# Block 0 of a fused S5 scan and GEGLU kernel: the second token tile goes last and is turned by DMA instead of on TensorE

## The chip, the cores and the metric

The kernel runs on one core of one Trainium2 chip. A core has TensorE (PE, matrix products; its loads of the stationary operand are listed apart as PEld), VectorE (DVE), ScalarE (ACT), GpSimd (POOL) and SyncE (SP), which here issues nearly all DMAs. Sixteen DMA engines move the data. TensorE's results land in PSUM, which has eight banks of 128 x 512 floats. The metric is the device time of one execution in microseconds; lower is better. The three runs of the kernel before took 176.82, 176.93 and 176.80 us, so the median is 176.82.

## The reference, cut to what matters

```
xn = (x - mean(x)) / sqrt(var(x) + 1e-5)                 # x: 2048 tokens x 512
dt = exp(log_dt);  Lam_bar = exp(dt * Lam)               # 512 complex states
Bu = xn @ (((Lam_bar - 1) / Lam)[:, None] * (B_re + i B_im)).T
h[t] = Lam_bar * h[t-1] + Bu[t]                          # scan over the tokens
A = 2 * real(h @ (C_re + i C_im).T) + xn * Dskip
B = (gelu(xn @ w_gate) * (xn @ w_up)) @ w_down           # hidden width 1376
out = x + A + B                                          # bf16
```

The result is the input plus a state-space branch plus a gated feed-forward branch, both fed by the layer-normed input.

## The kernel before, in words

The 2048 tokens are four blocks of 512, and a block is four tiles of 128 tokens. All of it lives in one large SBUF tensor, the arena, so the profile shows most operands as "arena". The hidden width 1376 is cut into tiles 0 to 9 of 128 columns and tile 10 of 96. The state branch makes B products (`BU`, L749), a scan on VectorE (`CHAIN`), and C products in the same PSUM bank as the down projection (`DN`, L885).

A program of operations with their reads and writes is built first. A planner orders them: TensorE and SyncE keep the order in which the operations are written; on VectorE, ScalarE and GpSimd a list scheduler with estimated durations and due times picks the order, and `order_behind` and `ch` pin some of them in a chain. Waits follow from the reads and writes.

*Two forms of the feed-forward products.* In the usual form (`GU`, L843) the weights are stationary and the normed, turned tokens `XNT` (features on partitions) stream through, giving hidden columns on partitions and 512 tokens in a row. `GU_rest` (L817) does the 96-column tile with the tokens stationary. Block 0 begins before its layer norm is known. There the tokens are only centred (L951, L962), turned on TensorE by `cent_T` (L684, four 128 x 128 turns a tile, copied to `XC` by ScalarE, L689), and kept stationary while gate and up weights stream (`GT_k`, L701, one k slice at a time as weights arrive; `GT_mm`, L712, all four k slices). The factor 1/sqrt(var) is put in later, by ScalarE's gelu (L721) and VectorE's product (L724). The result `H0`, tokens on partitions, covers hidden columns 0 to 895 in four units u of 256, 256, 256 and 128 columns, and is turned by DMA (`H0_T`, L730). Tiles 7 to 10 of block 0 are done in the usual form and need the normed tokens, `XNT[0]`, which `TR(0)` turns by DMA (L736, one DMA a token tile).

*Order on TensorE in block 0:* warm-up, turns and k slices of token tiles 0, 1 and 2 for units 0 and 1 (banks 0 to 5), the turn of token tile 3, then `GT_mm` for (token tile 3, units 0 and 1) and for all tiles with units 2 and 3, then `GU` tiles 7 to 9 (tile 7 in two token halves, so that its first half needs only the turned tokens of tiles 0 and 1), `GU_rest`, the B products of block 0, and the B products of block 1, whose first four units are cut in token halves too.

*Order on SyncE:* x tiles and the k slices of the first 512 gate and up columns (L497, L488); gate and up columns 512 to 895 (L493, 384 columns, rows of 768 bytes); gate and up columns 896 to 1375 (480 columns, rows of 960 bytes); the turn of the parameters (L515); `TR(0)`, four turns; x of block 1 (L482); the turns of B_re and B_im out of HBM (L526); Dskip (L535); x of block 2; `TR(1)`, four turns; and later `H0_T`, `TR(2)`, C, w_down and x of block 3. In block 0, ScalarE's queue loads two of the x tiles and the parameters.

*Order on VectorE around the change:* statistics of the x tiles, centring, root and reciprocal (L621, L627), the norms of `TR(0)`'s tiles (L634), the products of the token-stationary form (L724), and then the statistics of block 1. `GATE["hm"]` holds block 1's statistics behind the last product before them.

Of the kernel before, what the change touches and what calls it, by code (L numbers as in the profile page):

```python
# [365 lines left out]
def build(nc, ins, out):  # L366
    with ExitStack() as es:
# [16 lines left out]
        FC = [(0, 512), (512, 896), (896, F)]  # L384
        WGc = [Buf("WGc%d" % i, "sbx", 10 * i, 10 * i + 1) for i in range(KD + 2)]
        WUc = [Buf("WUc%d" % i, "sbx", 100 + 10 * i, 101 + 10 * i) for i in range(KD + 2)]
        wdeps = lambda Wc, ft: Wc[0:KD] if ft < 4 else [Wc[KD + (ft > 6)]]
# [30 lines left out]
        XT0 = XTk[0]  # L418
# [77 lines left out]
        def ld_x0(j, queue="sync", after=()):  # L496
            return S.dma(lambda e, j=j: e.dma_start(X[j].ap, x2[128 * j:128 * (j + 1), :]), 128 * 1024, writes=[X[j]], tag="ld_x0", queue=queue, after=after)  # L497
# [7 lines left out]
        ld_w(WG, WGc, ins["B_w_gate"], 1)  # L505
        ld_w(WU, WUc, ins["B_w_up"], 1)
# [22 lines left out]
        def load_W():  # L529
            ld_w(WG, WGc, ins["B_w_gate"], 2)  # L530
            ld_w(WU, WUc, ins["B_w_up"], 2)
# [172 lines left out]
        def GT_mm(j, u, bank):  # L704
            f0, f1 = FR[u]
            w = f1 - f0
            dst = PS[bank][:, 0:2 * w].rearrange("p (w f) -> p w f", w=2)

            def f(e):
                ins_ = None  # L710
                for k in range(KD):
                    ins_ = e.matmul(dst, XCd(j, k), WGU[:, :, k, f0:f1], start=(k == 0), stop=(k == KD - 1))  # L712
                return ins_
            PE(f, d_pe([2 * w] * KD), wdeps(WGc, 2 * u) + wdeps(WUc, 2 * u) + XCs[j], [BANK[bank]], "GT")

        def GT_evac(j, u, bank):
            f0, f1 = FR[u]
            w = f1 - f0
            GATE["nh"] = kk = (GATE["nh"] + 1) % 3
            sc, rb = rss[j]  # L720
            GATE["last_gelu"] = S.order_behind(ACT(lambda e: e.activation(GG[kk].ap[:, 0:w], PS[bank][:, 0:w], ACTF.Gelu_apprx_tanh, scale=sc),  # L721
                                                   d_act(w, 1), [BANK[bank], rb], [GG[kk]], "gelu"), GATE.get("last_gelu"))
            hp = Buf("H0_%d_%d" % (j, u), "sb", H0[j].lo + 2 * f0, H0[j].lo + 2 * f1)
            GATE["hm"] = S.order_behind(V(lambda e: e.scalar_tensor_tensor(H0[j].ap[:, f0:f1], PS[bank][:, w:2 * w], sc, GG[kk].ap[:, 0:w], ALU.mult, ALU.mult),  # L724
                                          d_dve_1x(w), [BANK[bank], GG[kk], rb], [hp], "hmul"), GATE.get("hm"))

        def H0_T():
            for j in range(4):
                wr = [Buf("HT0_%d_%d" % (ft, j), "sb", HTt[0][ft].lo + 256 * j, HTt[0][ft].lo + 256 * (j + 1)) for ft in range(7)]
                S.dma(lambda e, j=j: e.dma_start_transpose(HT[0].ap[:, 0:7, 128 * j:128 * (j + 1)], H0[j].ap),  # L730
                      3.5 * 224 * 1024, reads=[H0[j]], writes=wr, tag="tr_h0", issue=2100.0)

        def TR(b, js=range(4)):
            for j in js:
                tt = 4 * b + j
                S.dma(lambda e, b=b, j=j, tt=tt: e.dma_start_transpose(  # L736
                    XNT[b].ap[:, :, 128 * j:128 * (j + 1)], XN[tt % 8].ap),
                    1.6 * 128 * 1024, reads=[XN[tt % 8]], writes=[XTk[b][j]], tag="tr_x%d" % b, issue=1280.0)
# [67 lines left out]
        def GU_rest(b):  # L806
            k2, ft = b % 2, KF - 1
            f0, m = 128 * ft, FROWS[ft]
            for i in range(2):
# [10 lines left out]
                PE(f, d_pe([2 * m] * 8), [WGc[KD + 1], WUc[KD + 1]] + XTr(b), [BANK[bank]], "GR%d" % b)  # L820
# [11 lines left out]
        def GU(b, fts=None, halved=()):  # L832
# [14 lines left out]

            for ft in fts:
# [4 lines left out]
                banks[ft] = (next_bank(), next_bank())  # L853
                bg, bu = banks[ft]
                kk = (KF * b + ft) % 3
                for j0, j1 in (((0, 2), (2, 4)) if ft in halved else ((0, 4),)):
                    for (W, Wc, bank) in zip((WG, WU), (WGc, WUc), banks[ft]):
                        mm(ft, W, Wc, bank, 128 * j0, 128 * j1, XTr(b)[j0:j1])
# [10 lines left out]
        def DN(b, split=False, tail=None):  # L869
# [4 lines left out]
            def seed(j, c0=0, c1=D):  # L874
                tt, bank = 4 * b + j, banks[j]
# [22 lines left out]
            def store(j, c0=0, c1=D):  # L898
                tt = 4 * b + j
# [3 lines left out]
                V(lambda e: e.tensor_tensor(OUTB[ko].ap[:, c0:c1], PS[bank][:, c0:c1], XD[tt].ap[:, c0:c1], ALU.add),  # L903
                  d_dve_1x(c1 - c0), [BANK[bank], XD[tt]], [ob], "evO")
# [90 lines left out]
        ch(*stats(0, 3)); ch(sub(3))  # L995
        ch(recip(qb0, rq0))
        op, mn3, qb3, rq3 = root(0, 3, 4)
        ch(op)
        rss = [(rq0.ap[:, i:i + 1], rq0) for i in range(3)] + [(rq3.ap, rq3)]
        for j in range(2):  # L1000
            ch(norms(0, [j], mn0, rq0, 0))
        ch(recip(qb3, rq3))
        TR(0, [0, 1])
        ks(1, 2, [0, 1])
        ks(2, 2, [0, 1])
        for j in range(3):
            GT_k(3, j, 0, [0, 1])
            if j == 0:
                cent_T(3, 0, 4, 6)
# [3 lines left out]
        for (j, u), bank in zip([(3, 0), (3, 1), (0, 2), (0, 3), (1, 2), (1, 3), (2, 2), (2, 3), (3, 2), (3, 3)],  # L1013
                                (6, 7, 0, 1, 2, 3, 4, 5, 0, 7)):
            GT_mm(j, u, bank)
            GT_evac(j, u, bank)
        rstate["n"] = 2
        norms(0, [2], mn0, rq0, 0)
        norms(0, [3], mn3, rq3, 3)
        TR(0, [2, 3])  # L1020
        ld_x(1)
# [6 lines left out]
        GU(0, [7, 8, 9, 10], halved=[7])  # L1028
# [82 lines left out]
```

## Time and profile before

| | |
|---|---|
| median of 3 runs | 176.82 us (176.80 to 176.93) |
| the profiled execution | 177.26 us, span 175.9 us |
| instructions | 2549 |
| TensorE busy | 172.8 us, 98% of the span, 903 matmuls |
| VectorE, ScalarE, GpSimd busy | 159.7, 95.8, 10.7 us |
| HBM read, written | 6.46 MB, 2.10 MB |
| granted TensorE clock | 1.00 |

How to read it: the span is the time from the first to the last instruction of the profiled execution. Busy times are sums by engine; DMA-issuing instructions aren't counted in them. SPq is SyncE's queue, that is the instructions that issue DMAs; a DMA's landing is the time from its issue until its data is there. The chain of work that ended last is followed back from the last instruction: each step leads to what released it, or to the instruction before it on its engine. L numbers are lines of the kernel before; the changed kernel's lines lie 1 to 19 further down.

### The profile page before, as it was taken

What the parts mean: (1) busy time and instruction counts of PE and PEld (TensorE: products, weight loads), DVE (VectorE), ACT (ScalarE), POOL (GpSimd) and SP (SyncE); (2) the same over time, 40 slices, a digit from 0 to 9 for tenths busy, and PEclk for the clock granted to TensorE, in tenths of its full rate; (3) what the DMA queues carried; (4) which work ended last, traced back from release to release, by engine and by line L of the source; (5) the groups of instructions that cost most, each with busy time, mean ns of one, the idle gap of its engine ahead of it and who ended that gap; (6) DMA issues with size and microseconds to landing.
All of it is one profiled execution on the core that took longest, in us unless ns stands there. A gap on an engine that the chain in (4) does not pass through costs nothing.

```text
span 175.9 us, 2549 instructions
## 1 busy us (share of the span) xinstructions
PE 172.8 (98%) x903; PEld 85.4 (49%) x903; DVE 159.7 (91%) x279; ACT 95.8 (54%) x187; POOL 10.7 (6%) x24
## 2 busy tenths in 40 slices
PE   7999999999999999999999999999999999999995
PEld 2645664744544444444644444444464444444454
DVE  6797999987999989889899999989999899999941
ACT  5367668999766899383676793000667970000000
POOL 3132120211000000002200000000000000000000
DMA  5999989975899000002015000002004000000311
GB/s 144 281 322 154 216 136 203 174 132 114 162 270 270 11 0 2 0 30 75 18 33 112 5 0 4 0 0 89 30 0 34 0 0 0 0 0 4 119 62 60
DMA packets 32421, 14.36 MB, mean 82 GB/s; under 512 B 23737, under 2 KB 32409, under 8 KB 32409
## 3 DMA queue, kind: packets, MB, share of 16 engines
q1 hardware_dynamic: 31952, 13.84, 36.9%
q10 hardware_dynamic: 456, 0.36, 0.6%
q8 instruction: 7, 0.11, 0.3%
q14 instruction: 6, 0.04, 0.1%
HBM read 6.46 MB, written 2.10 MB: 49 GB/s over the span
## 4 chain that ended last, share of the span: by engine, by line
PE 95%; DMA 2%; SPq 1%; issue 0%; DVE 0%
PE PS L885 37%; PE PS L843 32%; PE PS L749 16%; PE PS L712 4%; PE PS L817 3%; PE PS L701 2%; DMA arena<-in_B_w_up_dram 2%; SPq L488 1%; PE PS L684 0%; SPq L497 0%; DVE arena L903 0%
## 5 line engine op out<-in xcount | busy, mean ns | idle before, releaser
L885 PE MATMUL PS<-arena 128*128 128x512 bf16 (+3 forms) x323 | 66.2, 366 | 0.0
L843 PE MATMUL PS<-arena 128*128 128x512 bf16 (+1 forms) x272 | 58.1, 373 | 0.0
L885 PEld LDWEIGHTS PS<-arena 128*128 128x128 bf16 (+1 forms) x323 | 30.8, 98 | 35.2
L843 PEld LDWEIGHTS PS<-arena 128*128 128x128 bf16 x272 | 26.5, 98 | 29.5
L787 DVE TENSOR_TENSOR_SCAN arena<-arena 128x512 bf16<-128x512 f32 x32 | 38.9, 1256 | 0.0
L859 ACT ACTIVATE arena<-PS 128x512 bf16<-128x512 f32 x33 | 19.8, 599 | 26.2 <-DVE arena L903 16.7
L749 PE MATMUL PS<-arena 128*128 128x512 bf16 (+1 forms) x144 | 28.3, 355 | 0.1
L863 ACT ACTIVATE arena<-PS 128x512 bf16<-128x512 f32 x33 | 19.8, 599 | 5.4 <-PE PS L843 5.4
L749 PEld LDWEIGHTS PS<-arena 128*128 128x128 bf16 x144 | 14.0, 98 | 13.7 <-DMA arena<-arena 0.6
L877 ACT ACTIVATE PS<-arena 128x512 f32<-128x512 bf16 (+2 forms) x17 | 9.6, 582 | 19.7 <-DVE arena L903 19.0
L758 ACT ACTIVATE arena<-PS 128x512 bf16<-128x512 f32 x32 | 17.6, 597 | 1.6 <-PE PS L749 1.6
L903 DVE TENSOR_TENSOR arena<-PS,arena 128x512 bf16<-128x512 f32 (+2 forms) x17 | 10.9, 654 | 6.4 <-PE PS L885 6.4
L865 DVE TENSOR_TENSOR arena<-arena 128x512 bf16<-128x512 bf16 x33 | 13.2, 419 | 2.1 <-ACT arena L863 2.0
L776 DVE TENSOR_TENSOR arena<-arena 128x4096 bf16<-128x4096 bf16 (+1 forms) x5 | 9.2, 1859 | 0.4 <-ACT arena L611 0.4
L799 DVE TENSOR_TENSOR arena<-arena 128x4096 bf16<-128x4096 bf16 x4 | 9.2, 2291 | 0.1
L774 DVE TENSOR_TENSOR arena<-arena 128x4096 bf16<-128x4096 bf16 (+1 forms) x5 | 9.2, 1861 | 0.0
L800 DVE TENSOR_TENSOR arena<-arena 128x4096 bf16<-128x4096 bf16 x4 | 9.1, 2287 | 0.0
L615 DVE BATCH_NORM_STATS2 arena<-arena 128x6 f32<-128x512 bf16 x12 | 7.8, 685 | 0.9 <-DMA arena<-in_A_x_dram 0.7
L721 ACT ACTIVATE arena<-PS,arena 128x256 bf16<-128x256 f32 (+1 forms) x16 | 6.5, 450 | 3.3 <-DVE arena L621 1.5
L712 PE MATMUL PS<-arena 128*128 128x512 bf16 (+1 forms) x40 | 7.1, 336 | 0.0
L701 PE MATMUL PS<-arena 128*128 128x256 bf16 (+1 forms) x36 | 6.2, 308 | 0.2 <-DMA arena<-in_B_w_up_dram 0.2
L724 DVE SCALAR_TENSOR_TENSOR arena<-PS,arena 128x256 bf16<-128x256 f32 (+1 forms) x16 | 6.2, 444 | 0.0
(95 smaller groups left out, 124.2 us busy)
## 6 DMA issues: line engine op xcount, KB each, us to landing
out_dram<-arena SPq DMA_DIRECT2D x15, 128.0 KB, 1.7
arena<-in_A_x_dram SPq DMA_DIRECT2D x3, 512.0 KB, 6.3
arena<-in_B_w_down_dram SPq DMA_DIRECT2D x1, 1280.0 KB, 8.8
arena<-in_B_w_gate_dram SPq DMA_DIRECT2D x4, 128.0 KB, 3.4
arena<-in_B_w_up_dram SPq DMA_DIRECT2D x4, 128.0 KB, 3.6
arena<-in_B_w_gate_dram SPq DMA_DIRECT2D x1, 480.0 KB, 6.8
arena<-in_B_w_up_dram SPq DMA_DIRECT2D x1, 480.0 KB, 7.6
arena<-arena SPq DMA_TRANSPOSE x25, 3.3
```

The lines of the kernel that those rows point to most:

```text
L701: PE(lambda e: e.matmul(dst, XCd(j, k), WGU[:, ws[0]:ws[-1] + 1, k, f0:f1], start=first, stop=k == KD - 1, skip_group_check=True), d_pe([w ...
L712: ins_ = e.matmul(dst, XCd(j, k), WGU[:, :, k, f0:f1], start=(k == 0), stop=(k == KD - 1))
L749: ins_ = e.matmul(PS[bank][:, 128 * j0:128 * j1], BBT[c][dk].ap[:, 128 * s:128 * (s + 1)], XNT[b].ap[:, dk, 128 * j0:128 * j1], start=(dk ...
L758: GATE["evBu"] = ACT(lambda e, bank=bank, k3=k3, s=s, c=c: e.activation(SSc[k3][s][c].ap, PS[bank][:, :], ACTF.Copy), d_act(512), [BANK[ba ...
L787: V(lambda e, g=g, rb=rb, init=init: e.tensor_tensor_scan(g.ap, rb, g.ap, init, ALU.mult, ALU.add), d_dve_scan(512), [g, PA[RRr]] + ([CARc ...
L843: ins_ = e.matmul(PS[bank][0:m, c0:c1], W.ap[:, dk, 128 * ft:128 * ft + m], XNT[b].ap[:, dk, c0:c1], start=(dk == 0), stop=(dk == KD - 1))
L859: GATE["last_gelu"] = ACT(lambda e, bg=bg, kk=kk, m=m: e.activation(GG[kk].ap[0:m, :], PS[bg][0:m, :], ACTF.Gelu_apprx_tanh), d_act(512), ...
L863: ACT(lambda e, bu=bu, kk=kk, m=m: e.activation(UPB[kk].ap[0:m, :], PS[bu][0:m, :], ACTF.Copy), d_act(512), [BANK[bu]], [UPB[kk]], "evU")
L865: V(lambda e, kk=kk, m=m, ft=ft, k2=k2: e.tensor_tensor(HTt[k2][ft].ap[0:m, :], GG[kk].ap[0:m, :], UPB[kk].ap[0:m, :], ALU.mult), d_dve_tt ...
L877: ACT(lambda e: e.activation(PS[bank][:, c0:c1], X[tt].ap[:, c0:c1], ACTF.Copy), d_act(c1 - c0), [X[tt]], [BANK[bank]], "seed")
L885: ins_ = e.matmul(PS[bank][:, c0:c1], l_[:, 128 * j:128 * (j + 1)], r_[:, c0:c1], start=False, stop=last and n == len(ops) - 1, skip_group ...
L903: V(lambda e: e.tensor_tensor(OUTB[ko].ap[:, c0:c1], PS[bank][:, c0:c1], XD[tt].ap[:, c0:c1], ALU.add), d_dve_1x(c1 - c0), [BANK[bank], XD ...
```

## The change

1. The x tiles of block 0 are loaded into slots in the token order 0, 2, 3, 1 (`TOK`). Slots 0 to 2 (token tiles 0, 2, 3) are centred and turned on TensorE as before. Slot 3 (token tile 1) is no longer centred and turned on TensorE: its token-stationary products read the normed tokens in `XNT[0]`, turned by DMA, and its gelu and product take no factor.
2. `TR(0)` is cut up: turns of slots 0 and 3 (token tiles 0 and 1), then the load of the last 480 up columns, then x of block 1, then the turns of slots 1 and 2.
3. The 384-column chunk of gate and up becomes two, of 256 and 128 columns (rows of 512 and 256 bytes).
4. The order of `GT_mm` changes: unit 2 of slots 0, 1, 2, unit 3 of slots 0, 1, 2, then all four units of slot 3.
5. `GU` tiles 7, 8 and 9 are all cut in token halves, and the first halves of all three come before the second halves.

```diff
-        FC = [(0, 512), (512, 896), (896, F)]
+        FC = [(0, 512), (512, 768), (768, 896), (896, F)]
...
-        XT0 = XTk[0]
+        TOK = (0, 2, 3, 1)
+        XT0 = [XTk[0][t] for t in TOK]
...
         def load_W():
-            ld_w(WG, WGc, ins["B_w_gate"], 2)
-            ld_w(WU, WUc, ins["B_w_up"], 2)
+            ld_w(WG, WGc, ins["B_w_gate"], 3)
...
                 for k in range(KD):
-                    ins_ = e.matmul(dst, XCd(j, k), WGU[:, :, k, f0:f1], start=(k == 0), stop=(k == KD - 1))
+                    xs = XCd(j, k) if j < 3 else XNT[0].ap[:, k, 128 * TOK[j]:128 * (TOK[j] + 1)]
+                    ins_ = e.matmul(dst, xs, WGU[:, :, k, f0:f1], start=(k == 0), stop=(k == KD - 1))
...
+            def both(ft, j0, j1):
+                for (W, Wc, bank) in zip((WG, WU), (WGc, WUc), banks[ft]):
+                    mm(ft, W, Wc, bank, 128 * j0, 128 * j1, XTr(b)[j0:j1])
+
+            for ft in halved:
+                banks[ft] = (next_bank(), next_bank())
+            for ft in halved:
+                both(ft, 0, 2)
             for ft in fts:
...
+                if ft in halved:
+                    both(ft, 2, 4)
+                else:
+                    banks[ft] = (next_bank(), next_bank())
+                    both(ft, 0, 4)
...
-        ch(*stats(0, 3)); ch(sub(3))
-        ch(recip(qb0, rq0))
+        ch(*stats(0, 3))
         op, mn3, qb3, rq3 = root(0, 3, 4)
         ch(op)
-        rss = [(rq0.ap[:, i:i + 1], rq0) for i in range(3)] + [(rq3.ap, rq3)]
-        for j in range(2):
-            ch(norms(0, [j], mn0, rq0, 0))
+        ch(recip(qb0, rq0))
+        rss = [(rq0.ap[:, i:i + 1], rq0) for i in range(3)]
+        ch(norms(0, [0], mn0, rq0, 0))
+        ch(norms(0, [1], mn0, rq0, 0))
         ch(recip(qb3, rq3))
-        TR(0, [0, 1])
+        ch(norms(0, [3], mn3, rq3, 3))
+        TR(0, [0, 3])
+        ld_w(WU, WUc, ins["B_w_up"], 3)
+        ld_x(1)
+        TR(0, [1])
         ks(1, 2, [0, 1])
         ks(2, 2, [0, 1])
         for j in range(3):
             GT_k(3, j, 0, [0, 1])
-            if j == 0:
-                cent_T(3, 0, 4, 6)
             GT_k(3, j, 1, [0, 1])
             for u in range(2):
                 GT_evac(j, u, acc(j, u))
-        for (j, u), bank in zip([(3, 0), (3, 1), (0, 2), (0, 3), (1, 2), (1, 3), (2, 2), (2, 3), (3, 2), (3, 3)],
-                                (6, 7, 0, 1, 2, 3, 4, 5, 0, 7)):
+        for (j, u), bank in zip([(0, 2), (1, 2), (2, 2), (0, 3), (1, 3), (2, 3), (3, 0), (3, 1), (3, 2), (3, 3)],
+                                (6, 7, 0, 1, 2, 3, 4, 5, 6, 7)):
             GT_mm(j, u, bank)
             GT_evac(j, u, bank)
-        rstate["n"] = 2
+        rstate["n"] = 0
         norms(0, [2], mn0, rq0, 0)
-        norms(0, [3], mn3, rq3, 3)
-        TR(0, [2, 3])
-        ld_x(1)
+        TR(0, [2])
...
-        GU(0, [7, 8, 9, 10], halved=[7])
+        GU(0, [7, 8, 9, 10], halved=[7, 8, 9])
```

## The prediction

> **What bounds the kernel now.** I read the page's shares of busy time first, then the chain that ended last in order of time, then who waited for whom, then the DMA queue of SyncE, and last what that queue moved in single stretches.
>
> ```profile
> PE 172.8 (98%) x903; PEld 85.4 (49%) x903; DVE 159.7 (91%) x279; ACT 95.8 (54%) x187; POOL 10.7 (6%) x24
> ```
>
> TensorE is busy 98% of the span, so only less TensorE work, or a stall that comes or goes, can move the time. The chain in order of time (start us, us, what), around the change:
>
> ```profile
> 9.75 0.34 PE PS L684 x4
> 10.09 1.08 PE PS L701 x5
> 11.16 6.93 PE PS L712 x40
> 18.09 5.20 PE PS L843 x32
> 23.29 1.32 PE PS L817 x16
> 24.61 6.91 PE PS L749 x32
> 31.52 0.12 issue
> 31.64 7.11 PE PS L749 x48
> ```
>
> TensorE runs without a break from the last turned tile (L684) over the token-stationary part (L701, L712), the weight-stationary tiles (L843, L817) and the B products of block 0, up to 31.52. There is a gap of 0.12 us, and then come the B products of block 1. From 31.64 to the end the chain is TensorE again without a gap. The waits say what the gap is:
>
> ```profile
> PEld PS L749 <- DMA arena<-arena: 0.6, 1, 0.6
> ```
>
> The weights for the products of block 1 waited 0.6 us for an SBUF-to-SBUF transfer: a turn of block 1's tokens (L736). SyncE's queue (start, us):
>
> ```profile
> 10.27 5.15 SPq L736 DMA_TRANSPOSE arena<-arena  x4
> 15.46 0.58 SPq L482 DMA_DIRECT2D arena<-in_A_x_dram  x1
> 16.09 3.22 SPq L526 DMA_TRANSPOSE arena<-in_A_B_re_dram  x1
> 19.35 3.67 SPq L526 DMA_TRANSPOSE arena<-in_A_B_im_dram  x1
> ...
> 24.17 2.40 SPq L736 DMA_TRANSPOSE arena<-arena  x1
> 26.62 1.27 SPq L736 DMA_TRANSPOSE arena<-arena  x1
> ```
>
> The last two are the turns of tokens 0 and 1 of block 1. The transfer view of the second alone:
>
> ```profile
> arena<-arena SPq DMA_TRANSPOSE x1, 4.9
> ```
>
> It lands at 26.62 + 4.9 = 31.55, and TensorE goes on at 31.64. A turn with nothing ahead of it lands 2.5 us after its issue (the least in the view of L736), so this one stood 2.4 us behind other transfers. **So a second limit lies under the first: SyncE's queue, of which everything up to 31.5 us is just in time.** How full it is (stretch, TensorE, its weights, VectorE, ScalarE, GpSimd, clock, DMA share, GB/s):
>
> ```profile
> 9.00:10.00 1.00, 1.00 (x9) 0.45 (x8) 0.86 (x6) 0.15 (x1) 0.84 (x3) 1.00 0.99 290
> 16.00:17.00 1.00, 1.00 (x8) 0.66 (x7) 0.73 (x3) 0.53 (x2) 0.16 (x1) 1.00 0.33 33
> 17.00:18.00 1.00, 1.00 (x9) 0.66 (x7) 0.96 (x4) 0.53 (x2) 0.00 (x0) 1.00 0.76 209
> 50.00:51.00 1.00, 1.00 (x6) 0.48 (x5) 0.92 (x1) 0.76 (x2) 0.00 (x0) 1.00 0.73 216
> ```
>
> From 5 to 16 us the DMA engines are full. Then there is a hole of 0.7 + 0.2 us where plain loads follow turns. The clock is 1.00 throughout.
>
> **The change part by part.**
>
> *Four turns less on TensorE.* The chain has them at 0.34 us. The copy out of PSUM that goes with them (0.59 us of ScalarE) and one centring on VectorE (0.35 us, L951) go too; neither is on the chain. All other token-stationary matmuls stay: 24 of 512 and 16 of 256 columns in L712 before and after. Gain: 0.34 us, if nothing waits.
>
> *Tiles 7, 8, 9 in halves (7 was so before).* Sixteen matmuls of 512 columns become 32 of 256. L749 gives 6.91/32 = 0.216 us for 512 columns; the mixed stretch of L843 gives (5.20 - 16 x 0.216)/16 = 0.109 us for 256. That is 32 x 0.109 against 16 x 0.216: +0.03 us. Their weight loads take 98 ns (the page's L843 PEld row) and still fit under 109.
>
> *The weight chunk of 384 columns becomes 256 + 128.* SyncE issues one load more ahead of the turns. Each such load takes 0.5 to 0.65 us there, so the parameter turn moves from 7.82 to about 8.4 and ends at 10.3. Turn 0 starts there, as before (10.27), since its normed tile is ready by about 10.1 (one centring less ahead of it). Its partner, tile 1, is normed by 11.4 and is issued at 11.6. Then come the late weight load (0.65), block 1's tokens (0.58) and the other two turns (1.27 each, L736's median), so that the turn of B_re is issued at 16.8 instead of 16.09: 0.7 us late on SyncE. What waits behind these issues on SyncE is the rest of that fence, down to block 1's turns.
>
> In the engines, 1024 rows of 768 bytes become 1024 of 512 and 1024 of 256. Prices, from three stretches of one kind each (8.5 to 9.5 us: 768 bytes; 11.5 to 12: 960 bytes; 24 to 24.5: 256 bytes, turned):
>
> ```profile
> DMA packets 376, 0.28 MB, mean 280 GB/s; under 512 B 12, under 2 KB 376, under 8 KB 376
> DMA packets 196, 0.18 MB, mean 362 GB/s; under 512 B 7, under 2 KB 196, under 8 KB 196
> DMA packets 568, 0.15 MB, mean 291 GB/s; under 512 B 568, under 2 KB 568, under 8 KB 568
> ```
>
> Sixteen engines make that 43, 41 and 14 ns a packet. No row has a plain packet of 512 or 256 bytes. At the lower end 256 costs 14 and 512 the middle, 29 ns: together 43, nothing added. At the upper end each piece costs what a plain packet costs (43, as 768 and 960 differ little): 43 ns x 1024/16 = 2.8 us added. I take 0.5 us, near the lower end, because the nearest row in size for half of the new packets is the cheap one.
>
> That row says that 256-byte pieces are cheap per packet. The Trainium skill, "DMA: Bandwidth & Descriptors", section Specifications, puts the least transfer for full line rate at 512 bytes and says that below it a read-modify-write is done; it speaks against the 128-column chunk. If that makes a 256-byte piece as dear as a 768-byte one, an estimate from this case's prices is 29 + 43 - 43 = 29 ns x 1024/16 = 1.9 us in place of 0.5, and the sum 178.7 in place of 177.3. The row is of turned packets from SBUF or HBM, so it doesn't refute this for plain ones.
>
> *The hole.* Plain loads follow turns as often as before. The first such hole cost 0.9 us; there the load was issued late (15.46). Where the load had been waiting in the queue (W_down behind C_im, 50 to 51) it cost 0.3. After the change the load waits in the queue (issued at 12.9, turns over at about 14.5). Bounds: 0.6 less, or no less; I take 0.2 less.
>
> *What is late next.* The DMA side gives +0.5 - 0.2 = +0.3, SyncE's side +0.7. Its B_re and B_im issues are stretched by the full queue (3.22 and 3.67 against 2.44 and 1.97 us for C), so part of its 0.7 is swallowed. I take the middle: **block 1's second turn lands 0.5 us later, at 32.05, and TensorE starts there at 32.14.**
>
> *TensorE up to there.* It reaches the token-stationary units at 10.82. The first needs the up half of the 256-column chunk. The last k load lands at 8.77 (4.98 + 3.8); before, 768 KB behind it took until 11.95 (5.95 + 6.0). For 512 KB in as many packets: 2/3 of 3.18 us, 10.9, or all of it, 11.95. I take 11.1, a new wait of 0.3 us. VectorE's products now stand behind four norms and start at 11.4; bank 0 is wanted at 12.8, when its product is done (11.8). The unit of tile 1 comes at 11.1 + 12 x 0.216 + 12 x 0.109 = 15.0. Its turn: the plain loads ended at 7.04 + 7.6 = 14.6; without the 480 KB moved back they ended at 6.50 + 6.8 = 13.3, and 0.5 on top makes 13.8. The second turn landed 1.0 behind them (11.53 + 4.1 = 15.6), so now at 14.8. No wait. The halves start at 18.0, and those of tokens 2 and 3 at 20.65; the late weights should land at about 17 and the late turns at 19.7. B_re lands at 16.09 + 7.6 + 0.5 = 24.2, wanted at 24.6. TensorE would reach block 1's products at 31.5: all its new waits, up to 0.6 us, lie under the turn's 32.14.
>
> *Behind it* nothing changes: the chain has no wait from 31.64 on. W_down, the next transfer TensorE needs, lands at 56.7 for use at 64.24, so 0.5 us is covered.
>
> **The sum.** 31.64 becomes 32.14: +0.5 us. The profiled execution took 177.26 us with a span of 175.9 (1.4 around it); it lies 0.44 above the median of the runs, 176.82. The span should be 176.4, and the median 176.82 + 0.5 = 177.3.
>
> **Rivals.**
> - *The whole gain is kept.* TensorE's 0.34 and the gap's 0.12 are all that can be won: -0.46, 176.4. It needs block 1's second turn to land by 31.1, 0.45 earlier, and no wait for the 256-column chunk. For it: the hole may shrink by 0.6. Against: one load more on a SyncE that never pauses after 10.27, and no byte less in the queue.
> - *A draw.* Small packets cost nothing, the hole shrinks a little, and the turn lands within 0.2 us of 31.55: 176.8. For it: 14 + 29 = 43 ns.
> - *Small packets are dear.* Their 1.9 us go through the queue to block 1's turn: 178.7. It decides from about 1 us on, when the wait for the chunk and for tile 1's turn also show.
> - *The halves do nothing.* If the late turns land by 18 us, halving tiles 8 and 9 buys nothing; it costs 0.03 us, and the time is the forecast's.
>
> **How the numbers follow.** The forecast's case (turn late by 0.2 to 0.9): 0.55. A draw: 0.15. The gain: 0.12. Dear packets: 0.18. A measurement of this kernel can't tell less than 0.2%, 0.35 us, from no change. Faster beyond it: most of the gain's case, 0.08. Same: the draw, the rest of the gain (0.04) and the low part of the forecast's case (0.13), 0.32. Slower: 0.42 + 0.18 = 0.60. The range, 176.5 to 178.7, leaves out the best part of the gain and the worst of the dear packets. The forecast's own is 177.0 to 177.7.
>
> **What would show it.** Right: the gap before the first products of block 1, waiting for a turn, grows from 0.12 to about 1 us less TensorE's earlier waits; a wait of about 0.3 us before the first token-stationary unit, on the up weights; the parameter turn starts at about 8.4 and B_re at 16.8; twelve turns on TensorE instead of sixteen; nothing new after 33 us. Wrong: no gap at block 1's products (then the queue had room, and the gain shows), a gap of over 0.5 us at tile 1's unit (then the turn was the wrong form), or packets of 256 bytes at over 30 ns.

## The result

The changed kernel takes 177.54 us (median of 22 executions, 176.84 to 179.12); the kernel before, run beside it, takes 176.95 (22 executions, 176.72 to 177.39). The ratio is 1.0034, with a 95% interval of 1.002 to 1.0048: a little slower, by 0.6 us. The profiled execution of the changed kernel took 177.41 us with a span of 176.1; that of before took 177.26 with 175.9. So the changed one was profiled near its median, and the other 0.3 above its median. What the two profiles differ by, 0.15 us, is less than what the medians differ by (0.59), and it has to be kept in mind below. All ratios leave out two executions of experiment 6 with a granted clock of 0.991 (181.14 and 181.60 us); every other execution shows 1.00.

TensorE's row on the page of the changed kernel:

```profile
PE 172.4 (98%) x901; PEld 87.7 (50%) x915; DVE 159.6 (91%) x278; ACT 94.5 (54%) x186; POOL 10.8 (6%) x24
```

The page counts 901 matmuls to 915 weight loads, and counted 903 to 903 before: 14 matmuls of this trace have no record (the program has 903 - 4 + 16 = 915). So its busy time, 0.4 us less than before, can't be compared. Where TensorE stands, the chain that ended last says, in order of time (start us, us, what):

```profile
7.72 0.22 PE PS L685 x4
...
10.91 6.93 PE PS L714 x40
17.84 2.62 PE PS L853 x24
20.46 0.04 issue
20.50 2.78 PE PS L853 x24
...
24.60 0.07 issue
24.67 6.85 PE PS L759 x31
31.52 0.15 issue
31.67 3.65 PE PS L759 x32
...
174.12 0.29 DVE arena L922
```

The part of the gain that the change promises is there: from the last turned tile (L685) to the token-stationary units (L714) it now takes 10.91 - 7.72 = 3.19 us, and took 11.16 - 7.59 = 3.57. But in place of one break there are two: 0.04 in the middle of the halved tiles and 0.15 ahead of the B products of block 1. The 0.07 ahead of the B products of block 0 is no break. Behind it stand 31 matmuls and not 32, and the line of the B products has two records too few:

```profile
L759 PE MATMUL PS<-arena 128*128 128x512 bf16 (+1 forms) x142 | 28.0, 355 | 0.3
L759 PEld LDWEIGHTS PS<-arena 128*128 128x128 bf16 x144 | 13.9, 98 | 13.8 <-DMA arena<-arena 0.6
```

With the 0.07 the stretch is 24.60 to 31.52, 6.92 us, and it was 6.91 before. So its first matmul ran and isn't recorded; the chain has more such gaps, of 0.05 each, further on. The last instruction starts at 174.12, and did at 174.09. The one wait for a transfer among these breaks is the old one, with the length that it had:

```profile
PEld PS L759 <- DMA arena<-arena: 0.6, 1, 0.6
```

SyncE's queue (start us, us, what):

```profile
13.06 0.58 SPq L494 DMA_DIRECT2D arena<-in_B_w_up_dram  x1
...
16.86 3.14 SPq L528 DMA_TRANSPOSE arena<-in_A_B_re_dram  x1
...
25.16 5.21 SPq L746 DMA_TRANSPOSE arena<-arena  x4
```

The first line is the load of the late up weights. The turn of B_re is issued at 16.86, 0.77 later than before (16.09). The turns of block 1 are issued from 25.16 on, against 24.17. The second of them, 1.24 further on, has this line in the transfer view:

```profile
arena<-arena SPq DMA_TRANSPOSE x1, 5.2
```

It lands at 26.40 + 5.18 = 31.58, 0.03 later than before. Of SyncE's delay nothing had reached its issue: it is issued at 26.40, and was at 26.62, because the issue of the first turn took 2.40 us before and about 1.2 now.

**What a break costs.** Before, the B products of blocks 0 and 1 took 6.91 + 0.12 + 7.11 = 14.14 us. Experiment 2, in which the break is gone, has the same 80 matmuls in one piece:

```profile
24.82 13.85 PE PS L751 x80
```

So the break of 0.12 cost 0.29, some 0.17 us more than the gap in the chain. The traces have a number that fits: a matmul of 512 columns is 379 ns long (groups by shape) while the next starts 216 ns after it, and one of 256 columns 272 and 109. Each runs 0.163 us into the next one, and the chain's gap begins only where the last has ended. The ends are modelled in these profiles, so this is argued, not shown. In the same way the halved tiles take 2.62 + 0.04 + 2.78 = 5.44 with the break and 5.24 without (experiment 8 below). This gives a measure that is free of what happened in the first 10 us. From the start of the first token-stationary unit to the end of block 1's B products a kernel without a stop needs 6.93 + 5.24 + 1.32 + 13.85 = 27.34 us in the changed form and 27.30 in the old one (5.20 for 5.24). What is above it was lost in stops:

| profiled execution | first unit starts | block 1's B products end | lost in stops |
|---|---|---|---|
| before | 11.16 | 38.75 | 0.29 |
| changed | 10.91 | 38.78 | 0.53 |
| changed, second (experiment 4) | 11.10 | 38.86 | 0.42 |
| changed, third (experiment 11) | 10.98 | 39.06 | 0.74 |

Behind it nothing differs: 174.09 - 38.75 and 174.12 - 38.78 are both 135.34 us. So the time of any of these kernels is the start of the first unit, plus the stops, plus 165.9 us (177.41 - 10.91 - 0.53 = 165.97, 177.26 - 11.16 - 0.29 = 165.81).

**Who is late.** For each transfer in a row, when TensorE would want it without a stop there, and when it landed (issue plus time to landing in the transfer views):

| us | before wants, lands | changed | second | third |
|---|---|---|---|---|
| up weights of the first unit that isn't k-sliced | 12.89, 11.95 | 10.91, 10.60 | 11.10, 10.68 | 10.98, 10.63 |
| last turn of block 0 | 18.96, 16.65 | 20.46, 20.36 | 20.65, 20.61 | 20.53, 20.45 |
| B_re | 24.61, 23.65 | 24.60, 24.39 | 24.84, 24.65 | 24.69, 24.48 |
| second turn of block 1 | 31.52, 31.55 | 31.52, 31.58 | 31.75, 31.66 | 31.61, 31.86 |

Before, one transfer was just in time and the others had 0.9 us or more to spare. Now all four have 0.4 us or less, and all four stand behind each other on SyncE and in the same DMA engines.

### The profile page after: what moved, and what is told of

It is laid out like the page before. It is cut to its first block, busy times and chain, and to the rows that moved or that the text cites. A ratio compares the mean times of both kernels' runs of the same rounds, so it can differ in the third digit from the quotient of the medians.

```text
span 176.1 us, 2565 instructions
## 1 busy us (share of the span) xinstructions
PE 172.4 (98%) x901; PEld 87.7 (50%) x915; DVE 159.6 (91%) x278; ACT 94.5 (54%) x186; POOL 10.8 (6%) x24
## 2 busy tenths in 40 slices
DMA packets 33477, 14.37 MB, mean 82 GB/s; under 512 B 24792, under 2 KB 33464, under 8 KB 33464
## 4 chain that ended last, share of the span: by engine, by line
PE 98%; issue 1%; DVE 0%
PE PS L904 37%; PE PS L853 32%; PE PS L759 16%; PE PS L714 4%; PE PS L702 3%; PE PS L827 3%; PE PS L953 2%; PE PS L685 1%; DVE arena L922 0%; PE PS L960 0%
## 5 line engine op out<-in xcount | busy, mean ns | idle before, releaser
L853 PEld LDWEIGHTS PS<-arena 128*128 128x128 bf16 x288 | 28.1, 98 | 28.4 <-issue 0.3
L759 PEld LDWEIGHTS PS<-arena 128*128 128x128 bf16 x144 | 13.9, 98 | 13.8 <-DMA arena<-arena 0.6
L896 ACT ACTIVATE PS<-arena 128x512 f32<-128x512 bf16 (+2 forms) x17 | 9.6, 581 | 19.7 <-DVE arena L922 19.0
L714 PE MATMUL PS<-arena 128*128 128x512 bf16 (+1 forms) x40 | 7.1, 336 | 0.0
L827 PE MATMUL PS<-arena 128*128 128x192 bf16 x64 | 5.9, 246 | 0.0
L726 ACT ACTIVATE arena<-PS,arena 128x256 bf16<-128x256 f32 (+1 forms) x12 | 4.8, 446 | 2.0 <-PE PS L702 1.5
```

What stands on the lines that cost most here:

```text
L714: ins_ = e.matmul(dst, xs, WGU[:, :, k, f0:f1], start=(k == 0), stop=(k == KD - 1))
L759: ins_ = e.matmul(PS[bank][:, 128 * j0:128 * j1], BBT[c][dk].ap[:, 128 * s:128 * (s + 1)], XNT[b].ap[:, dk, 128 * j0:128 * j1], start=(dk ...
L827: ins_ = e.matmul(dst, XNT[b].ap[:, dk, 128 * j:128 * (j + 1)], WGU[:, :, dk, f0:f0 + m], start=(dk == 0), stop=(dk == KD - 1))
L853: ins_ = e.matmul(PS[bank][0:m, c0:c1], W.ap[:, dk, 128 * ft:128 * ft + m], XNT[b].ap[:, dk, c0:c1], start=(dk == 0), stop=(dk == KD - 1))
```

## The experiments

All times of the kernel before are from executions beside those of the experiment. "Last instruction" is the start of the last VectorE instruction of the profiled execution, 174.09 before and 174.12 after the change.

**1. The changed kernel, with block 1's first two turns ahead of Dskip and of x of block 2.** This takes the load off the transfer that I had named as the bound. `load_D` holds the two loads that are moved.

```diff
-        TR(1)
+        TR(1, [0, 1])
+        load_D()
+        TR(1, [2, 3])
```

> The changed kernel, but on SyncE the turns of tokens 0 and 1 of block 1 go ahead of Dskip and of x of block 2 (behind B_im). Theory A (block 1's second turn lands at about the moment TensorE wants it, 31.6 against 31.5, and in slower executions later, so it eats the 0.34 us): that turn lands about 3 us earlier, the gap before the products of block 1 goes, and the kernel gains the 0.34 and the gap: about 176.4 to 176.6, that is 0.3 to 0.5 below the kernel before. Theory B (the loss arises earlier, at block 0's late turns or at B_re, which this edit doesn't move): still 177.3 to 177.6, with the spread of the changed kernel. Theory C (the loss lies behind 32 us): no better than the changed kernel.

Measured: 178.12 us (177.39 to 178.58, 12 executions) against 177.13; ratio 1.0047 (1.003 to 1.0063). The turns of block 1 land at 26.2 and 27.4, 4 us early, and TensorE doesn't stop there. It stops for block 0's late turns; the chain (start us, us, what) and one line of the waits:

```profile
15.13 5.92 DMA arena<-arena
21.05 0.14 issue
21.18 2.78 PE PS L855 x24
...
174.48 0.29 DVE arena L924
```

```profile
PE PS L855 <- DMA arena<-arena: 0.8, 1, 0.8
```

The edit moves nothing that is issued ahead of these turns, so that they landed at 21.05 in place of 20.36 is not the doing of the queue's order. The late weights, ahead of them, even landed earlier (17.25 for 17.92). In between stands x of block 1: its first part landed at 18.48 and its last at 20.05, and about then one of the engines also had a fetch of the program's own instructions, 16 KB, from 18.06 on for 0.93 us (the queue view of 17.9 to 19.1: packets, MB, share):

```profile
q8 instruction: 1, 0.02, 4.9%
```

In the changed kernel's profile that fetch came at 21.81, behind the late turns. It is likely what made them late here: the second of them lands 5.92 us behind its issue, and 4.70 to 5.14 in the five profiles with the same queue up to there and a later fetch (the changed kernel, experiments 4, 5, 6 and 11). No run moved the fetch by itself. The median is above what any of the three theories gave. What follows: block 1's turn isn't the one bound of the changed kernel. The late turns of block 0 can cost as much.

**2. The kernel before, with the same edit.**

> The kernel before with the same edit alone. Theory A: only the gap of 0.12 us can go, so 0.1 to 0.2 below the kernel before, 176.7 to 176.85. If the gap is not the turn's: no change. If x of block 2, now later, holds up VectorE's statistics and through them the scan: above 177.

Measured: 177.23 us (176.81 to 178.52, 12 executions) against 177.13; ratio 1.0013 (0.9994 to 1.0033). The break is gone (the line of 13.85 us above), and the last instruction starts at 174.02; but the first unit starts at 11.38 in this execution, so the 0.29 doesn't show in its time. It doesn't show in the median either: the interval has no room for a gain of 0.29 us, and the forecast of 176.7 to 176.85 missed. Whether most executions of the kernel before have no such break, or the edit costs as much elsewhere, isn't shown.

**3. The changed kernel, with the old order of the queue:** both loads of 480 columns ahead of the turns, x of block 1 behind all four.

```diff
             ld_w(WG, WGc, ins["B_w_gate"], 3)
+            ld_w(WU, WUc, ins["B_w_up"], 3)
...
-        ld_w(WU, WUc, ins["B_w_up"], 3)
-        ld_x(1)
         TR(0, [1])
...
         TR(0, [2])
+        ld_x(1)
```

> The changed kernel with SyncE's old order: both 480-column loads ahead of the turns of block 0, x of block 1 behind all four. If the cut queue (late up columns and x of block 1 ahead of the late turns) costs B_re and block 1's turns their time: 0.2 to 0.4 faster than the changed kernel, B_re landing near 23.7. If the cut queue is needed for slot 3's turn: a wait of 0.5 us or more before slot 3's first unit at about 14.7, and a time of 177.5 or more.

Measured: 177.76 us (177.56 to 178.27, 11 executions) against 177.13; ratio 1.003 (1.0016 to 1.0044). The turn of token tile 1 now lands at 16.05, and TensorE stands in its token-stationary units:

```profile
12.53 3.52 DMA arena<-arena
16.05 0.05 issue
16.09 3.20 PE PS L715 x16
```

It waits for the turn for 1.2 us. Behind this stop nothing else stops it. So the load that the change puts behind the first two turns has to stand there for the DMA-turned form, and there it stands ahead of the late turns.

**4. The changed kernel again, unchanged.**

> The changed kernel as it is, for a second profile and a time on the same chip. Its first profile shows block 0's late turns (20.36 against 20.46 wanted), B_re (24.39 against 24.6) and block 1's second turn (31.58 against 31.5) all just in time, and its runs spread from 176.84 to 179.12. Theory A: a slower execution shows its loss as a longer gap at block 1's products alone. Theory B: it shows it at B_re or at block 0's late turns. Time 177.2 to 177.8.

Measured: 177.37 us (176.83 to 178.71, 12 executions) against 177.13; ratio 1.0025 (1.0001 to 1.0048). The profiled execution took 177.41 us as the first did, with another set of stops:

```profile
18.03 2.62 PE PS L853 x24
20.65 0.09 issue
20.74 2.78 PE PS L853 x24
...
24.84 14.02 PE PS L759 x80
```

A larger stop stands at the late turns. The B products have a hidden one (14.02 for 13.85): by its single matmuls one starts at 31.40 and the next, the first of block 1, at 31.75, where 0.22 lie between others. So the two places are those of the first profile; how much is lost at which of them changes from execution to execution.

**5. The changed kernel, with the chunk of 384 columns whole.**

```diff
-        FC = [(0, 512), (512, 768), (768, 896), (896, F)]
+        FC = [(0, 512), (512, 896), (896, F)]
```

> The changed kernel with the 384-column chunk whole again (rows of 768 bytes), all else as changed. Theory A (TensorE is paced by transfers that land just in time): the first token-stationary unit now waits for the whole up chunk, landing at 11.5 to 12 against 10.8 wanted, so 0.7 to 1.2 us of wait there, most of it under the later waits: 177.5 to 178.3. If small packets were the cost: block 0's late turns and B_re land 0.5 us earlier than in the changed kernel and the time falls by 0.3 to 0.5.

Measured: 178.12 us (177.79 to 178.17, 4 executions) against 176.92; ratio 1.0066 (1.0052 to 1.0081). SyncE has one load less to issue, and everything behind it is earlier: the late weights are issued at 12.37 and not at 13.06 and land at 16.92 and not at 17.92, the late turns land at 19.47 for 20.36, B_re at 22.85 for 24.39, block 1's second turn at 30.06 for 31.58. TensorE doesn't stop for any of them. But it stands for the chunk, which lands at 11.97:

```profile
5.93 6.04 DMA arena<-in_B_w_up_dram
11.97 0.14 issue
12.10 7.09 PE PS L714 x40
```

The wait was forecast, at 0.7 to 1.2 us. So the split is needed: its first piece lands at 10.60 and its last at 11.45 in the changed kernel, the whole chunk at 11.97. Its price is the issue, by this comparison of two executions. In the kernel before, the same chunk at 11.95 cost nothing, because token tile 3's k-sliced units came first.

**6. The changed kernel, with only tile 7 in halves.**

```diff
-        GU(0, [7, 8, 9, 10], halved=[7, 8, 9])
+        GU(0, [7, 8, 9, 10], halved=[7])
```

> The changed kernel with tile 7 alone in halves. Theory A: the second half of tile 7 wants block 0's late turns at about 18.8, they land at 20.4, so TensorE stands for about 1.6 us there, and as it then reaches block 1's products at about 33 that wait goes: 178.1 to 178.6. If the halves do nothing (the rival of the prediction): 177.2 to 177.6.

Measured: 178.28 us in the profiled execution and 179.72 in one more, against 176.92; ratio 1.0123 (1.0089 to 1.0156). TensorE stands for the late turns, which land at 19.96:

```profile
15.23 4.73 DMA arena<-arena
19.96 0.14 issue
20.10 4.49 PE PS L853 x24
```

The halves are needed; they put off the need for the late turns by 1.75 us (16 matmuls of 0.109) and this is just enough to hide most of it.

**7. The changed kernel, with x of block 1 behind all four turns of block 0, and block 1's first two turns ahead of Dskip and x of block 2.**

> The changed kernel with x of block 1 behind all four turns of block 0, and with block 1's turns of tokens 0 and 1 ahead of Dskip and x of block 2. Theory A (the gain is eaten at two places, block 0's late turns and block 1's second turn): the late turns land at 18.5 to 19.3 for use at 20.4, block 1's turns at 26 to 28 for use at 31.2, TensorE runs without a gap from the weights on, and the kernel is 0.4 to 0.6 faster than before: 176.4 to 176.7, with less spread than the changed kernel. If a third place holds it (B_re, landing at 24.4 or later for 24.2): no faster than before.

Measured: 177.97 us (177.82 to 179.26, 6 executions) against 176.92; ratio 1.008 (1.0057 to 1.0103). Block 0's late turns land at 17.5 and 18.0, block 1's first two at 26.65 and 28.58. Now its other two come behind x of block 2:

```profile
33.87 0.14 issue
34.00 5.36 PE PS L761 x32
```

The wait went one transfer on. The forecast, a gain and no gap from the weights on, missed.

**8. The changed kernel, with x of block 1 behind all four turns of block 0, and nothing else.**

```diff
-        ld_x(1)
         TR(0, [1])
...
         TR(0, [2])
+        ld_x(1)
```

> The changed kernel with x of block 1 behind all four turns of block 0 and nothing else. Theory A: the late turns are early, but block 1's second turn still lands at about 31.6 or a little later and TensorE waits for it there: the gap grows to 0.3 to 0.5 us, and the time is that of the kernel before within 0.2, 176.9 to 177.2. If block 0's late turns alone were the loss: as fast as the run with both edits.

Measured: 177.16 us (176.64 to 177.67, 12 executions) against 176.92; ratio 1.0013 (1.0001 to 1.0026). The profiled execution is the fastest of the twelve, 176.64 us, and shows the whole gain:

```profile
10.72 6.93 PE PS L714 x40
17.65 5.24 PE PS L853 x48
...
24.21 13.91 PE PS L759 x80
...
173.46 0.29 DVE arena L922
```

The first unit starts at 10.72, 0.06 us is lost in stops, and the last instruction starts 0.63 us earlier than before. The late turns land at 18.70 and 19.23, B_re at 23.50, block 1's turn at 30.87. So the mechanism of the change can pay 0.6 us when no transfer is late. But the median stays where it was; it lies in the forecast's 176.9 to 177.2, though the gap of 0.3 to 0.5 us that the forecast had at block 1 isn't there.

**9. As 8, with all four turns of block 1 ahead of Dskip and x of block 2.**

> The changed kernel with x of block 1 behind all four turns of block 0, and with all four turns of block 1 ahead of Dskip and x of block 2. Theory A (TensorE loses to turns that land just in time, and to nothing else): every turn has at least 1 us to spare, TensorE has no gap from the weights to the end, and the median lies 0.3 to 0.6 below that of the kernel before, with no execution over 177.3. Rival (x of block 2 and Dskip, now landing at 33 to 34, hold up VectorE's statistics and scan, and the down projection of block 0 waits): a new wait on VectorE at 31 to 34 and a gap on TensorE at about 64 or later; 177 or more.

Measured: 177.35 us (176.58 to 178.9, 12 executions) against 176.98; ratio 1.0037 (1.0016 to 1.0059). The turns land at 26.6 to 30.5. The wait is at B_re, in front of which nothing was changed against experiment 8, where it landed at 23.50:

```profile
16.78 7.78 DMA arena<-in_A_B_re_dram
24.56 0.05 issue
24.61 14.03 PE PS L761 x80
```

One thing that does differ is the fetch of 16 KB: it starts at 16.42 in experiment 8 and at 22.50 here, between B_re's issue and its landing (see the last section).

**10. As 8, with Dskip alone behind block 1's turns.**

> The changed kernel with x of block 1 behind all four turns of block 0, and with Dskip alone behind block 1's turns. Theory A: block 1's second turn lands 0.5 to 1.3 us earlier than in the run with x of block 1 behind alone (30.9 there), so it has about 1 us to spare, and the median falls to 176.4 to 176.8. If Dskip's slow start just moves to x of block 2 behind B_im: the turn lands where it did, and the median is 177.1 as there.

Measured: 177.13 us (176.67 to 177.63, 12 executions) against 176.98; ratio 1.0005 (0.9991 to 1.002). The late turns land at 19.21 and 19.68, B_re at 23.73, block 1's turns between 27.88 and 31.23, and none is waited for. So the second turn of block 1 is 1.5 us earlier than in experiment 8, as forecast, and the median (176.4 to 176.8 forecast) doesn't follow. What is left is the first unit, whose weights land at 10.68 (the timeline's bracket: us idle before, and what ended it):

```profile
10.81 1.46 PE L716 MATMUL PS<-arena 128*128 128x512 bf16 x6 [0.28 <-DMA arena<-in_B_w_up_dram]
```

**11. The changed kernel a third time, one execution.**

> The changed kernel as it is, for a third profile. Theory A: its waits lie at block 0's late turns and at block 1's second turn, and their sum with the 0.17 us that a stop costs behind it gives its place between 176.8 and 178.7.

Measured: 177.60 us. The chain:

```profile
31.61 0.34 issue
31.95 7.11 PE PS L759 x48
...
174.40 0.29 DVE arena L922
```

This execution shows the forecast's own picture: block 1's second turn lands at 26.50 + 5.37 = 31.86, 0.31 later than before, TensorE goes on at 31.95 and not at 31.64, and the last instruction starts 0.31 later.

**12. As 10, with the widths of the second and the third unit exchanged,** so that the first unit needs 128 columns and not 256.

```diff
-        FC = [(0, 512), (512, 768), (768, 896), (896, F)]
+        FC = [(0, 512), (512, 640), (640, 896), (896, F)]
...
-        FR = ((0, 256), (256, 512), (512, 768), (768, 896))
+        FR = ((0, 256), (256, 512), (512, 640), (640, 896))
```

> As e10_x_behind_dskip_late, with the widths of the second and third unit of token tile 0 exchanged, so that the first token-stationary unit needs a load of 128 columns (as a 128-column chunk 1b landed at 11.45 behind 1a's 10.60, it is the smaller of the two, and now goes first) in place of 256. Theory (the gains of the change are given back at whichever just-in-time transfer lands last, and the first unit's chunk, landed at 10.68 with a wait of 0.28, is the last such place left in e10): the chunk lands near 10.2, no wait at the first unit, none at the late turns, B_re or block 1's turns; the last instruction ends at 173.3 to 173.6 and the median is 0.2 to 0.5 below the kernel before (176.4 to 176.8). Rival (the rest of the time lies ahead of 10 us, in the loads of the first weights and x, which no edit here touches): no wait at the first unit either, but the median stays within 0.15 of the kernel before, and executions differ by where the first 10 us end. Second rival: the third unit's chunk, now the wider one, lands too late and the wait moves to it (0.2 or more, second token-stationary unit).

Measured: 177.20 us (176.87 to 177.65, 12 executions) against 177.12; ratio 1.0002 (0.9991 to 1.0013). No stop is left in the chain:

```profile
5.43 2.90 PE PS L704 x20
...
11.52 7.00 PE PS L716 x40
...
25.08 13.85 PE PS L761 x80
```

Yet the last instruction starts at 174.27. All of it comes from ahead of the first unit, which starts at 11.52 and not at 10.72: the twenty k-slice products of L704 took 2.90 us, and 2.33 in the changed kernel's profile. No engine and no transfer is waited for there. The products themselves were slower; the last section shows it. The rival's number held (within 0.15 of the kernel before), the theory's didn't.

No version beat the kernel before. The lowest ratios, those of experiments 10 and 12, can't be told from 1.

## Why the prediction was right, and where it wasn't

The time (177.3 forecast, 177.54 and 177.37 measured) and the direction came out as written. The kind of reason was right too: TensorE's gain is real, and in the profiles it is given back to transfers on SyncE's queue that are just in time. But that the number came out is in part luck. The sum put +0.5 us at one place, block 1's second turn. The three profiles show that turn 0.03 to 0.31 late and the rest of the loss at block 0's late turns, where the prediction had no wait, and with TensorE's earlier start they end 0.15 to 0.34 us above the profile of before, where the medians moved by 0.59 and 0.24. Point by point:

*Four turns less: right.* 3.57 us became 3.19, against 0.34 forecast.

*The halves: right.* 5.24 for 5.20 us, +0.04 against +0.03. That they would be needed, against the rival in which they do nothing, experiment 6 shows.

*Small packets: the mis-sized term.* I had put +0.5 us, with 0 and 2.8 as ends. Two stretches of the changed kernel's transfers, of half a microsecond each, where the 512-byte and where the 256-byte rows move (8 to 8.5 and 9.5 to 10 us):

```profile
DMA packets 282, 0.14 MB, mean 279 GB/s; under 512 B 10, under 2 KB 282, under 8 KB 282
DMA packets 535, 0.15 MB, mean 292 GB/s; under 512 B 497, under 2 KB 535, under 8 KB 535
```

Sixteen engines make that 16 x 500/282 = 28 and 16 x 500/535 = 15 ns a packet, together 43: the lower end, as the turned packets of the trace of before had it, and what one of 768 bytes cost. In the engines the split added nothing. By the rule of the Trainium skill ("DMA: Bandwidth & Descriptors", Specifications, the 512-byte minimum) I had worked out 1.9 us; rows of 256 bytes out of HBM moved at the same 292 GB/s here, so the measurement decides against it for this kernel. (The 178.7 that went with it added the 1.9 us whole; by the middle of the two sides that the forecast takes, it would have been 178.0.)

*SyncE's side: right at B_re's issue, wrong at the second turn's.* The turn of B_re started at 16.86, forecast 16.8. The parameter turn, forecast at 8.4, started at 9.14: the issue of the load ahead of it took 1.44 us and not 0.5 to 0.65. Experiment 5, with one issue less, shows what that is worth further on: 1.0 us at the late weights, 0.9 at the late turns, 1.5 at B_re and at block 1's second turn, between these two executions. But I had block 1's second turn at 32.05, as the middle of +0.3 and +0.7. It was issued 0.22 us earlier than before, so that of the 0.7 nothing was left, and it landed at 31.58, 31.66 and 31.86 in three executions: 0.03 to 0.31 late and not 0.5.

*The hole and the late weights: wrong.* I had made the hole 0.2 us shorter and had the late weights at 17, starting when the turns ahead were over (14.29). They landed at 17.92, 18.11 and 17.92, 4.84 to 5.07 behind their issue. What decides is the load behind them. With x of block 1 next in the queue they landed 4.5 to 5.1 us behind their issue (six profiles: the changed kernel, experiments 1, 4, 5, 6 and 11); with block 0's late turns next, 3.9 to 4.1 (experiments 7 to 10 and 12), at 16.6 to 17.5. In experiment 8 that move is the only edit. In experiment 10 they were issued at 13.09 and the turns ahead were over at 14.29, as in the changed kernel, and they landed at 17.00. So x of block 1, which the change put between the late weights and the late turns, costs the weights ahead of it about 0.9 us, and the late turns come behind both. The prediction gave it no effect on the weights. This is the step that failed, because of what hangs on it:

*"No wait" at the late turns: wrong.* They were forecast at 19.7 and came at 20.36 to 20.61, wanted at 20.46 to 20.65. TensorE stopped there in all three executions, for 0.04 to 0.09 us, and 0.20 to 0.25 by the length of the halved tiles. With x of block 1 behind them they land at 17.5 to 19.7, and TensorE doesn't stop there (experiments 7 to 10 and 12). B_re, forecast at 24.2, came at 24.39 to 24.65 and had no wait that shows, as forecast. So the stops that I had summed up at one place, +0.5 at block 1, lay at two, with 0.42 to 0.74 in all, against 0.29 before.

*The first unit's wait of 0.3: not in the changed kernel's profiles, seen in experiments 9 (0.20) and 10 (0.28).* The weights came at 10.60, as 0.5 less than I had taken makes it. Whether there is a wait depends on when TensorE gets there, 10.5 to 11.5 us in the runs here.

*Behind 33 us nothing new: right,* 135.34 us in both.

Experiments 1, 3, 5, 6, 7 and 9 show that no one wait is the cause. Each takes the pressure off one transfer, or puts it on another, and TensorE then stops at that one or at the next. Experiments 8 and 12, with 0.06 and 0.07 us lost in stops, show that the order and the size of the loads can take them out.

What stays open: the median. In the profiles the first unit starts at 10.91, 11.10 and 10.98 in the changed kernel and 11.16 before, and the stops cost 0.13 to 0.45 more than before. That makes 177.41, 177.41 and 177.60 against 177.26. The medians differ by more (0.59 and 0.24 us in two sets of executions), since the kernel before is mostly faster than in its profile, and the changed one often slower: eight of its first 22 executions took 177.98 us or more, and none of the 22 of before took over 177.39. By the sum above, a median of 176.95 needs a first unit and stops of 11.1 us together (11.45 in its profile), and the 177.20 of experiment 12 needs 11.3, though its profile has no stop. No trace shows those executions. Either TensorE gets to the first unit at other times in them, or their transfers land at other times; which, these runs don't tell.

## What to carry to other kernels

Before TensorE's work is cut at a place where one transfer is just in time, list the transfers behind it too, with when each is wanted and when it lands; a gain is worth no more than the least slack among them, and taking 0.3 us of work away takes 0.3 us of slack from all. A stop costs more than the gap that the chain shows (0.17 us more here), so several small ones weigh like one large one. Count matmuls against weight loads before a gap is read as a stop: a matmul without a record leaves one too. A single profile isn't enough to compare kernels by a few tenths of a microsecond: take out what happened ahead of the part in question, and look at a second execution before one gap is named as the bound.

## What the runs showed that I had not expected

**TensorE runs at half its rate at first, for a time that differs by execution.** Groups of instructions by shape, for the stretch from 5.3 to 6.8 us (xcount | busy us, mean ns of one | idle), first of experiment 8, then of experiment 12:

```profile
L702 PE MATMUL PS<-arena 128*128 128x256 bf16 x16 | 2.0, 273 | 0.0
```

```profile
L704 PE MATMUL PS<-arena 128*128 128x256 bf16 x8 | 1.8, 406 | 0.0
```

The same product of 256 columns takes 273 ns in one and 406 in the other, and 16 start in the stretch against 8. The table of stretches gives both a granted clock of 1.00 (experiment 8, then 12; the third number from the end):

```profile
5.30:6.80 1.50, 1.50 (x16) 1.22 (x14) 0.96 (x3) 0.31 (x1) 0.00 (x0) 1.00 1.03 311
```

```profile
5.30:6.80 1.50, 1.50 (x10) 1.06 (x8) 0.99 (x4) 0.49 (x1) 0.00 (x0) 1.00 0.95 302
```

By the durations of the single products, the change from the slow to the fast rate comes at about 3.4 us in the profile of before, at 5.5 in that of the changed kernel, at 3.4 and 5.7 in experiments 4 and 11 (the same program), at 3.4 in experiment 8 and at 6.8 in experiment 12. Between the last two the first unit starts 0.80 us later, which is more than all that the change was about. So what I had read as late weights or as a lucky start is in part this. The Trainium skill ("TensorE: Matmul & The Clock Gate", Part 1: The HAM clock gate) tells of a clock at half rate until a window of about 3.4 us has been busy, a window that runs free of the kernel's start. The first matmul here is at 0.8 us, and the changes lie between 3.4 and 6.8, a spread of 3.4 us: the spread agrees with a window of that length, and not with the 0.5 us to either side that the page also gives. The earliest change comes some 2.6 us behind the first matmul, sooner than a whole window could have been busy; why, no run here shows.

**A short break costs 0.17 us more than the chain's gap.** 14.14 us against 13.85 for a gap of 0.12 (before, experiment 2), and 6.92 + 0.34 + 7.11 = 14.37 for a gap of 0.34 (experiment 11). I had counted gaps at their length, so that the whole gain would have been 0.34 + 0.29 = 0.63 us and not 0.46.

**A fetch of instructions goes with late transfers, and moves with the program.** 16 KB, 0.93 to 1.17 us on one engine. It began at 20.06 in the profile of before, at 21.81, 21.89 and 22.51 in three of the changed kernel, and between 16.42 and 22.50 in the experiments. Experiments 7 to 10 and 12 have the same order of SyncE's queue from the first turns to B_im, and fall into two groups:

| us | fetch starts | second late turn, issue to landing | B_re lands |
|---|---|---|---|
| experiments 8 and 10 | 16.42, 17.17 | 4.74, 4.72 | 23.50, 23.73 |
| experiments 7, 9 and 12 | 20.58, 22.50, 20.10 | 3.21, 3.33, 3.33 | 24.53, 24.56, 24.58 |

Where the fetch falls in the time of the late turns, they take 1.4 to 1.5 us more; where it falls in that of B_re, B_re lands 0.8 to 1.1 us later (in experiment 12 it is also issued 0.4 to 0.8 later than in the others). Experiment 5, with another queue, doesn't fit the second half: its fetch at 20.94 falls in B_re's time too, and B_re lands 6.76 us behind its issue, as in 8 and 10 (7.06, 6.81). So an edit of the order of instructions, far behind a transfer, can come with a change of a microsecond in its landing. No run moved the fetch alone, so that it is the cause is likely and not shown.
